# Which buffer holds the weight sums of the last two pairs of column blocks in the second batch's first layer

## The chip, the cores and the metric

The kernel runs on one core of a Trainium2 chip. The metric is the time on the device in microseconds (us), as the median of several runs. One execution was also taken by the hardware profiler; it gives the profile and the trace that are read here. TensorE does matrix products, VectorE (DVE in the profile) and GpSimd (POOL) do operations on tensors, ScalarE (ACT) does copies and activation functions, and SyncE (SP) issues the transfers (DMAs). SBUF is the memory on the core, PSUM holds results of TensorE, and DRAM is the memory off the core.

## The reference

Attention with a mask by cluster is followed by a two-layer network with the activation x·sigmoid(1.702x). Only the second part matters here:

```python
def _moe_ref(x, w_in, w_out) -> np.ndarray:
    h = x @ w_in
    g = h * (1.0 / (1.0 + np.exp(-1.702 * h)))
    return (g @ w_out).astype(np.float32)
```

x has 3072 rows (4 batches of 768 tokens) and 512 columns, w_in is 512 x 2048, and w_out is 2048 x 512. All is float32.

## The kernel before

The kernel has one long first part, the attention of all four batches (until about 340 us of the span), and then the two layers batch after batch (b = 0 to 3). The order of all instructions on each engine is the order in which the program writes them; no scheduler changes it.

**Products by seven.** Both layers multiply by the scheme of Strassen and Winograd: the matrices are cut in 2 x 2 parts, and seven products of sums of these parts take the place of eight products. So sums of weights and sums of inputs have to be made. Batches 0 and 1 use seven products in the first layer. Batches 2 and 3 apply the scheme twice there (`first49`), with 49 products, and need more sums of weights.

**The first layer of batch 1** is the stage of the change (lines 1380 to 1396). It works through eight blocks of 128 hidden columns, in the order TURN = 0, 4, 1, 5, 2, 6, 3, 7. I call the position in this order n, so n = 0 to 7. Two neighbours, n = 0 and 1, n = 2 and 3, and so on, are a pair. For each n the program writes, in this order:

- `first7_psum` (L922): seven products on TensorE (L928), in three banks of PSUM, with additions on VectorE (L884) and copies and gelus on ScalarE (L936, L942, L946, L949) between them. The products take the weight sums S[1], S[2] and S[4] of this n; S[3] lies in the weights' own place.
- for even n from 2 on, `inner_w` (L995) of the pair before: eight operations on VectorE that make the inner sums for the later batches from this pair's S, in the buffer `Zb[4]`, and then four DMAs (L1018), issued by SP, that copy these sums and S itself to DRAM (`kept_i`): 896 KB from `Zb[4]`, then 384 KB of the first S and twice 128 KB of the second S of the pair.
- `sums_w1(n + 2)` (L977): the three weight sums of the block two places later, for n + 2 up to 7. The sums of n = 0 and 1 were made by GpSimd at the end of batch 0; those from n = 2 on are made by VectorE.
- `after7` (L959): one subtraction of the block before, and for blocks f from 4 on four operations of `start_t`.
- two steps of `pend`, which store the rest of batch 0's output while there is any.

After the last n, `after7` and `inner_w` of the last pair follow, and then the second layer (`second49`), with seven groups k = 0 to 6 of seven products.

**Where the sums lie.** `wq` is a ring of two tiles named W (128 partitions x 768 elements). The sums of n = 0 and 1 lie in its two tiles. For n from 2 on a slice of six rows of 128 in `Zb[2]` or `Zb[1]` is used; these are views of `Z_of[2]` and `Z_of[1]`, which the second layer needs for sums of its own weights. They were saved to DRAM (`kept_z`) and are loaded again by `move_z` (L969) in the second layer of batch 1. `1 + n // 2 % 2` gives 2 for n = 2 and 3, 1 for n = 4 and 5, and 2 again for n = 6 and 7.

**Waits.** The program writes no waits by hand. From the tiles that each instruction reads and writes, the language puts in the waits for semaphores: a write to a slice waits for all earlier reads of it, by engines and by DMAs. A new tile of the ring waits for what used the tile two before it. Later users of the ring are `first49` of batches 2 and 3.

On VectorE `sums` always shows as L618, and `add` as L884.

Of the kernel before, what the change touches and what calls it, by code (L numbers as in the profile page):

```python
# [38 lines left out]
def fast(  # L39
# [576 lines left out]
    def sums(engine, todo):  # L616
        for o, a, op, b in todo:
            engine.tensor_tensor(out=o, in0=a, in1=b, op=(  # L618
                ALU.add if op == "+" else ALU.subtract))
# [3 lines left out]
    def A_in(row, col, f):  # L623

        at = (row * FB + f) * P
        return w_in[:, 2 * col:2 * col + 2, at:at + P]
# [350 lines left out]
    def sums_w1(n):  # L977

        if n >= FB:
            return  # L980
        f = TURN[n]
        if n < 2:
            S = wq.tile([P, 3, 2, P], FP32, name="W")
        else:
            S = Zb[1 + n // 2 % 2][:, n % 2 * 6:n % 2 * 6 + 6].rearrange(
                "p (i c) n -> p i c n", c=2)
        w_of[FB + f] = {1: S[:, 0], 2: S[:, 1], 3: A_in(1, 0, f), 4: S[:, 2],
                        0: S}
        S = w_of[FB + f]
        A11, A12, A22 = A_in(0, 0, f), A_in(0, 1, f), A_in(1, 1, f)  # L990
        sums(nc.gpsimd if n < 2 else nc.vector, (
            (S[2], A22, "-", S[3]), (S[1], S[2], "+", A11),
            (S[4], A12, "-", S[2])))
# [385 lines left out]
    for b in range(B):  # L1379
        if b == 1:  # L1380
            done = None
            for n, f in enumerate(TURN):
                made_w = w_of[FB + f][0]
                first7_psum(b, f, *XT)
                if n % 2 == 0 and done:
                    inner_w(*done)
                sums_w1(n + 2)
                if n:
                    after7(TURN[n - 1])
                if n % 2 == 0:  # L1390
                    one = made_w
                else:
                    done = f - FQ, (one, made_w)
                do(pend, 2)
            after7(FB - 1)
            inner_w(*done)
        if b > 1:
            rest = first49(*XT)
        for f in range(FB if b == 0 else 0):
            first7(b, f, *XT)  # L1400
            if f + 2 < FB:
                sums_w(f + 2)
            else:
                sums_w1(f + 2 - FB)
            if f:
                after7(f - 1)
            if b == 0 and f < 3:
                for n in range(3 * f, min(3 * f + 3, FB)):
                    sums_z((nc.gpsimd, nc.vector, nc.vector)[n % 3], n)
            if b == 0 and f in (3, 4):  # L1410
                for i in ORDER[0:4] if f == 3 else ORDER[4:]:
                    turn_w(i)
            if b == 0 and f >= 3:
                for k in {3: (0,), 4: (1, 2), 5: (3,), 6: (4,), 7: ()}[f]:
                    keep_w(k, spare_y())
                if 5 <= f < 7:
                    load_sums(f - 5)
# [510 lines left out]
```

## Time and profile before

| What | us |
|---|---|
| median of three runs | 894.72 |
| lowest, highest | 894.64, 895.08 |
| the profiled execution's own time | 894.73 |
| its span, first to last instruction | 892.6 |
| first layer of batch 1, from its first matmul to the second layer's first | 476.24 to 556.10 |

The profile's times are counted from the start of the span. "Busy" is the time an engine works; the idle time before an instruction is shown together with what ended it, written as <- and the instruction that released it. PEclk is the share of the full clock that TensorE was granted. The chain of waits says what the last instruction waited for, followed back to the beginning. Its first line is

```profile
PE 95%; DVE 2%; DMA 1%; ACT 0%; issue 0%; SPq 0%; DVEq 0%; ACTq 0%
```

So the end of the program is set by TensorE for 95% of the span. The waits of SP's own queue between 500 and 620 us show when the copies of L1018 could be issued:

```profile
SPq L1018 <- DVE Z L618: 53.8, 4, 21.8
SPq L835 <- PE b L1254: 19.3, 4, 7.2
```

The columns after the colon are the total time, the number of waits and the longest. The four waits of L1018 are for the sums that are copied.

### The profile page before, as it was taken

Reading aid. Unit: us, or ns where it says so; the run is one execution under the profiler, and the core shown is the slowest. Engines: PE = TensorE matmul, PEld = TensorE weight load, DVE = VectorE, ACT = ScalarE, POOL = GpSimd, SP = SyncE. Lnnn points to the kernel's source line nnn. Section 1 sums busy time; section 2 is a strip of 40 time slices with the busy share of each in tenths; the row PEclk is TensorE's granted clock in tenths of the full one; section 3 lists DMA queues with packets and bytes.
Section 4 is the critical chain, followed back from the end, with each engine's and each line's share of the span. In section 5 each row is a group of like instructions: output and inputs, shape, how many; then the busy total and the mean of one; then the engine's idle time right before and its main releaser. Section 6 shows DMA issues by size and latency. Waiting matters only on the chain.

```text
span 892.6 us, 18197 instructions
## 1 busy us (share of the span) xinstructions
PE 874.7 (98%) x6910; PEld 605.1 (68%) x6910; DVE 728.1 (82%) x1241; ACT 394.8 (44%) x868; POOL 429.3 (48%) x393
## 2 busy tenths in 40 slices
PE   8999999999999999999999979999999999999996
PEld 3444444444444445557997546999887999887995
DVE  4899898999999996998997645799656899665894
ACT  3677767777777764322112323111444212444211
POOL 6889999999999997693220000134000134000120
PEclk9999999999999999999999999999999999999999
DMA  9755566666655320035643311747511447501523
GB/s 175 134 105 104 103 121 150 140 131 137 137 130 121 86 67 19 0 119 167 224 140 102 98 71 71 282 142 267 141 54 48 166 142 265 171 25 48 185 66 97
DMA packets 183185, 110.48 MB, mean 124 GB/s; under 512 B 153528, under 2 KB 161712, under 8 KB 180528
## 3 DMA queue, kind: packets, MB, share of 16 engines
q1 hardware_dynamic: 182832, 109.09, 45.2%
q8 instruction: 57, 0.93, 0.5%
q14 instruction: 40, 0.33, 0.1%
q10 hardware_dynamic: 256, 0.13, 0.1%
HBM read 83.05 MB, written 26.14 MB: 122 GB/s over the span
## 4 chain that ended last, share of the span: by engine, by line
PE 95%; DVE 2%; DMA 1%; ACT 0%; issue 0%; SPq 0%; DVEq 0%; ACTq 0%
PE b L1254 29%; PE s L492 14%; PE o L557 14%; PE b L1129 8%; PE b L893 8%; PE m L1084 7%; PE b L928 7%; PE s L515 3%; PE m L574 3%; PE m L348 1%; DVE Z L618 1%; DMA in<-in_k_dram 1%; DMA kept_i<-Z 0%; PE s L506 0%; PE o L296 0%
## 5 line engine op out<-in xcount | busy, mean ns | idle before, releaser
L541 POOL TENSOR_TENSOR sum<-sum,A 128x384 f32<-128x384 f32 x252 | 265.3, 1089 | 23.0 <-ACT A L523 21.3
L618 POOL TENSOR_TENSOR Y<-y,Y 128x768 f32<-128x768 f32 x24 | 58.0, 2431 | 392.8 <-DVE y L884 368.9
L523 ACT ACTIVATE A<-s 128x768 f32<-128x768 f32 x192 | 146.2, 808 | 85.8 <-PE s L515 66.3
L492 PE MATMUL s<-T,T 64*64 64x384 f32 x1536 | 143.1, 487 | 0.0
L557 PE MATMUL o<-A,inv 64*64 64x384 f32 x1536 | 141.2, 483 | 0.0
L884 DVE TENSOR_TENSOR G<-b,G 128x384 f32<-128x384 f32 x128 | 68.4, 554 | 53.7 <-PE b L928 30.8
L492 PEld LDWEIGHTS s<-T,T 64*64 64x64 f32 x1536 | 54.9, 132 | 69.1 <-ACT A L523 35.8
L618 DVE TENSOR_TENSOR G<-G 128x768 f32<-128x768 f32 (+1 forms) x84 | 101.1, 1230 | 0.2
L557 PEld LDWEIGHTS o<-A,inv 64*64 64x64 f32 x1536 | 58.3, 133 | 38.4 <-issue 33.3
L1254 PE MATMUL b<-G,w_out 128*128 128x192 f32 x320 | 55.9, 326 | 0.0
L1142 ACT COPY G<-b 128x384 f32<-128x384 f32 x64 | 30.4, 480 | 52.2 <-PE b L1129 52.2
L1254 PEld LDWEIGHTS b<-G,w_out 128*128 128x128 f32 x320 | 52.7, 190 | 1.1
L1254 PE MATMUL b<-E,Wz 128*128 128x192 f32 x288 | 50.3, 326 | 0.0
L1254 PEld LDWEIGHTS b<-E,Wz 128*128 128x128 f32 x288 | 47.3, 190 | 0.3 <-DVE E L618 0.3
L515 PE MATMUL s<-rows,rows 64*64 64x384 bf16 x720 | 45.5, 323 | 0.0
L515 PEld LDWEIGHTS <-rows 64*64 64x64 bf16 x720 | 22.9, 107 | 32.8 <-issue 32.7
L1254 PE MATMUL b<-G,Wz 128*128 128x192 f32 x224 | 41.0, 326 | 0.0
L1254 PE MATMUL b<-G,Z 128*128 128x192 f32 x224 | 39.0, 326 | 0.0
L541 POOL TENSOR_TENSOR sum<-A 128x384 f32<-128x384 f32 x32 | 37.3, 1185 | 0.0
L1254 PEld LDWEIGHTS b<-G,Wz 128*128 128x128 f32 x224 | 37.2, 190 | 0.0
L1254 PEld LDWEIGHTS b<-G,Z 128*128 128x128 f32 x224 | 36.8, 190 | 0.0
L898 ACT ACTIVATE G<-G 128x384 f32<-128x384 f32 x32 | 16.1, 523 | 46.4 <-DVE G L884 44.9
(234 smaller groups left out, 1682.2 us busy)
## 6 DMA issues: line engine op xcount, KB each, us to landing
Wz<-kept_w SPq DMA_DIRECT2D x78, 256.0 KB
Z<-kept_z SPq DMA_DIRECT2D x9, 1024.0 KB
raw<-in_moe_w_in_dram SPq DMA_DIRECT2D x16, 512.0 KB
raw<-in_moe_w_out_dram SPq DMA_DIRECT2D x16, 512.0 KB
Z<-kept_i SPq DMA_DIRECT2D x8, 1024.0 KB
inv<-in_v_dram SPq DMA_DIRECT2D x16, 384.0 KB
in<-in_q_dram SPq DMA_DIRECT2D x60, 96.0 KB
in<-in_k_dram SPq DMA_DIRECT2D x60, 96.0 KB
```

The lines of the kernel that those rows point to most:

```text
L492: nc.tensor.matmul(out=ps[c:c + D, a, 0:HALF], lhsT=T[p, 1][rows, kt * P + c:kt * P + c + D], rhs=T[p, 0][rows, h * HALF:(h + 1) * HALF], ...
L515: nc.tensor.matmul(out=s_of[u][c:c + D, a, :], lhsT=rows_of[1, p % 2][rows, kt * P + c:kt * P + c + D], rhs=rows_of[0, p % 2][rows, h * HA ...
L523: nc.scalar.activation(out=A_of[u], in_=s_of.pop(u), func=AF.Exp, scale=SCALE)
L541: nc.gpsimd.tensor_tensor(out=sum_of[g][:, a], in0=(A_of[u - 1] if kt == 1 else sum_of[g])[:, a], in1=A_of[u][:, a], op=ALU.add)
L557: nc.tensor.matmul(out=o_of[g][a * D:(a + 1) * D, r, 0:HALF], lhsT=v_in[p][rows, a, kt, :], rhs=A[rows, a, :], start=(kt == 0), stop=(kt = ...
L618: engine.tensor_tensor(out=o, in0=a, in1=b, op=(ALU.add if op == "+" else ALU.subtract))
L884: nc.vector.tensor_tensor(out=o, in0=p, in1=a, op=ALU.add)
L893: nc.tensor.matmul(out=ps[:, 0:HALF], lhsT=a[:, c], rhs=x(c), start=(c == 0), stop=(c == 1))
L928: nc.tensor.matmul(out=ps, lhsT=a[:, c], rhs=x(c), start=start and c == 0, stop=(c == 1), skip_group_check=True)
L1084: nc.tensor.matmul(out=whole_of[j][m][:, 0:HALF], lhsT=a[:, c], rhs=x(c), start=n == 1 and c == 0, stop=c == 1, skip_group_check=True)
L1129: nc.tensor.matmul(out=ps[i][:, h * QT:(h + 1) * QT], lhsT=a(o), rhs=M[o][n], start=n in (1, 2, 5) and h == 0, stop=True, skip_group_check ...
L1254: nc.tensor.matmul(out=ps, lhsT=A[n][:, f], rhs=M[n][:, f], start=start and f == 0, stop=(f == FQ - 1), skip_group_check=True)
```

## The change

The sums of n = 6 and 7 are put into the ring `wq` instead of `Zb[2]`. They are made by the same engine as before, since the line that chooses the engine is unchanged.

```diff
         f = TURN[n]
-        if n < 2:
+        if n not in range(2, 6):
             S = wq.tile([P, 3, 2, P], FP32, name="W")
         else:
             S = Zb[1 + n // 2 % 2][:, n % 2 * 6:n % 2 * 6 + 6].rearrange(
                 "p (i c) n -> p i c n", c=2)
```

With this, the sums of n = 6 take the ring's tile that held n = 0, and those of n = 7 the tile that held n = 1. The products of n = 6 and 7, `inner_w` of the last pair and its three copies of S read W instead of `Zb[2]`. The number of instructions on TensorE, VectorE, ScalarE and GpSimd is the same, and so is their order. On SP, the reload of `Z_of[2]` no longer waits for the last pair's three copies of S; the three loads of Wz behind it take over these waits.

## The prediction

> **What bounds the kernel now.** I read the page first, then the busy times of the eight column blocks of the edited stage, then the waits of that stage, then its timeline, one engine after another. The page says that TensorE is the bound almost everywhere:
>
> ```profile
> PE 874.7 (98%) x6910; PEld 605.1 (68%) x6910; DVE 728.1 (82%) x1241; ACT 394.8 (44%) x868; POOL 429.3 (48%) x393
> ...
> PE   8999999999999999999999979999999999999996
> ```
>
> One slice of the 40, the 24th (513 to 536 us), drops to 7. The start, the end and this slice are the only weak ones. Slice 24 lies in the second batch's first layer. I cut this stage at the first matmul of each block n = 0 to 7 (476.24, 485.27, 494.30, 503.33, 513.02, 522.05, 538.03, 547.07, end 556.10) and asked for busy times by stretch; these are n = 2, 3 and 5:
>
> ```profile
> core 0: us, PE busy (x) PEld busy (x) DVE busy (x) ACT busy (x) POOL busy (x), PEclk, DMA share, GB/s
> ...
> 494.30:503.33 9.03, 9.03 (x30) 5.32 (x29) 4.18 (x10) 3.40 (x8) 0.00 (x0) 1.00 0.20 44
> 503.33:513.02 9.69, 9.29 (x29) 5.24 (x28) 7.43 (x20) 3.38 (x8) 0.00 (x0) 1.00 0.42 162
> ...
> 522.05:538.03 15.98, 10.85 (x29) 6.04 (x28) 7.71 (x21) 3.41 (x8) 0.00 (x0) 0.89 0.26 98
> ```
>
> The first number is the length. A block is 9.03 us when TensorE never waits. Blocks 3 and 5 do the same matmuls behind the same kind of VectorE work, yet block 3 takes 9.69 and block 5 takes 15.98. The waits of this stage name one DMA and one long hole:
>
> ```profile
> PE b L928 <- ACT G L949: 5.5, 2, 5.1
> DVE Z L618 <- DMA kept_i<-Z: 4.6, 1, 4.6
> ```
>
> The timeline of TensorE shows the hole in block 5 and its small sister in block 3, and how slowly TensorE resumes (one product is x4 in the records; durations overlap, so I use differences of starts):
>
> ```profile
> 508.49 1.45 PE L928 MATMUL b<-Tx,w_in 128*128 128x384 f32 x4
> 510.34 1.56 PE L928 MATMUL b<-x,Z 128*128 128x384 f32 x4 [0.40 <-ACT G L949]
> 511.73 1.45 PE L928 MATMUL b<-Tx,w_in 128*128 128x384 f32 x4
> ...
> 527.21 1.45 PE L928 MATMUL b<-Tx,w_in 128*128 128x384 f32 x4
> 533.79 2.93 PE L928 MATMUL b<-x,Z 128*128 128x384 f32 x4 [5.13 <-ACT G L949]
> 536.51 1.69 PE L928 MATMUL b<-Tx,w_in 128*128 128x384 f32 x4
> ```
>
> The timeline of all engines at the hole shows the chain that ends it:
>
> ```profile
> 529.34 0.43 DVE L618 TENSOR_TENSOR Z<-w_in 128x256 f32<-128x256 f32 x1 [4.64 <-DMA kept_i<-Z]
> ...
> 532.26 0.55 DVE L884 TENSOR_TENSOR G<-b,G 128x384 f32<-128x384 f32 x1
> 532.85 0.52 ACT L936 ACTIVATE G<-G 128x384 f32<-128x384 f32 x1 [6.25 <-DVE G L884]
> 533.28 0.46 ACT L949 COPY G<-b 128x384 f32<-128x384 f32 x1
> ```
>
> The first row is the first sum of `sums_w1(6)`. It overwrites six rows of `Zb[2]` that hold pair 2's sums (n = 2), and the copy of these rows to DRAM (L1018) was issued only at 524.72, as soon as `inner_w(1)` had finished. Behind it on VectorE stand two more sums, four operations of `after7`/`start_t`, and the addition of L884 at n = 5. ScalarE's gelu waits for that addition, L949's copy stands behind the gelu, and TensorE's product with S[4] (L953) may not write the bank that L949 still reads.
>
> **What the Trainium skill says.** "DMA: Bandwidth & Descriptors", section "Queues, rings and completion order": on a DMA engine the increment of a semaphore lands only after every earlier write of that engine. So the wait for the 384 KB copy also carries the 896 KB copy issued just ahead of it. The trace agrees: by stretches of 1 us the DMA engines moved 229, 423, 354 and 374 kB from 525 on, the two copies are 1311 kB, reached at about 528.8, and VectorE went on at 529.34. "TensorE: Matmul & The Clock Gate", section "Part 1": the array falls to half clock after an idle window of about 3.4 us and returns after a busy one. The trace agrees: after 5.13 us idle it shows 0.50, after 0.40 us none:
>
> ```profile
> 528.60:533.80 5.20, 0.07 (x2) 0.01 (x1) 3.40 (x10) 0.89 (x2) 0.00 (x0) 0.98 0.19 63
> 533.80:536.50 2.70, 2.70 (x4) 1.51 (x5) 0.53 (x1) 0.52 (x1) 0.00 (x0) 0.50 0.00 0
> ...
> 509.00:513.00 4.00, 3.60 (x11) 1.82 (x11) 1.95 (x5) 1.89 (x4) 0.00 (x0) 1.00 0.46 164
> ```
>
> **The change part by part.** (1) Removed: the first sum of `sums_w1(6)` no longer waits for the copy of `Zb[2]`. It now waits for pair 1's copy (n = 0) out of the ring's first place, issued from 506.39 in a row of three. The DMA engines fall idle at 511, after 115 + 401 + 401 + 369 + 286 = 1572 kB by stretches of 1 us, which is all four copies of the pair:
>
> ```profile
> 510.00:511.00 1.00, 0.66 (x2) 0.49 (x3) 0.56 (x1) 0.38 (x2) 0.00 (x0) 1.00 0.87 286
> 511.00:512.00 1.00, 1.00 (x4) 0.57 (x3) 0.07 (x1) 0.43 (x1) 0.00 (x0) 1.00 0.00 1
> ```
>
> That is 13 us before the sum is reached; even with 0.5 us from last byte to release (528.8 to 529.34) it is free. The two other users are earlier still: TensorE's last product with the ring's tiles starts at 491.72, `inner_w(0)` reads them until 504.3. (2) What is late next: VectorE's own work. Block 3 shows it: the same 8 operations of `inner_w`, 3 sums and `after7` without a DMA wait leave a hole of 0.40. On VectorE the two passes run in step, 18.72 us apart: L884 at 502.24 and 520.96, `inner_w` at 502.71 and 521.44. So the first sum, at 505.88 in the first pass, would start at 505.88 + 18.72 = 524.60 instead of 529.34, 4.74 us earlier. (3) On the path: from start to start, block 5 against block 3:
> - last matmul before the hole to first after it: 533.79 - 527.21 = 6.58 against 510.34 - 508.49 = 1.85: 4.73 less (the DMA wait);
> - first group after the hole: 2.72 against 1.39: 1.33 less (half clock);
> - second group to the next block: 538.03 - 536.51 = 1.52 against 513.02 - 511.73 = 1.29: 0.23 less (clock recovering).
>
> Sum 4.73 + 1.33 + 0.23 = 6.29 us, which is 15.98 - 9.69. (4) Moved: the sums for n = 6, 7 are written to W and read from there by TensorE, `inner_w(3)` and three copies. Counts and engines are the same: 6 sums on VectorE at about 0.42 us. VectorE's reads of W (Z<-W, 0.415 to 0.426 us) and of Z (0.414 to 0.426) don't differ. That it writes sums of this shape to W isn't shown; with 128x192 it is, in the next stage: 0.346 to 0.351 us for W, 0.345 to 0.347 for p. I take nothing; the bound is 10% of three sums, 0.13 us, either way. n = 7's first sum waits for the ring's second place, copied with the first, so the same 13 us and more cover it. (5) SP: the reload of `Z_of[2]` (issued 568.46, first used at 583.39 in the fourth product of the second layer) loses its wait on the last pair's copies; the three Wz loads behind it take over those waits, and they wait for TensorE until 573.19 anyway, later than copies issued by 564.27. The reload stays behind that of `Z_of[4]`, so nothing moves; without that cover it would have to slip by some 10 us to matter. The next stage writes the ring's tiles (`first49`) from 622.5, 58 us after the last copy is issued. (6) After 538.03 TensorE is not idle until the last matmuls near 883, and everything follows TensorE, not a fixed time: the 6.29 us should come off whole.
>
> Against the profiled execution's own time, 894.73 (span 892.6 and 2.13 around it): 894.73 - 6.29 = 888.44. The median of the plain runs is 894.72, so I say **888.4**.
>
> **Rivals.**
> A, the forecast, 888.4: 84%. Spread 0.5 either way: 0.13 for W, the rest for the 0.44 us between the lowest and highest run before.
> B, only the wait goes: the clock still dips once in this stage, so the 1.56 us stay. 894.72 - 4.73 = 890.0. For it: block 3 resumes with 1.56 instead of 1.45. Against it: the clock reads 1.00 there. 6%.
> C, more than A: block 5 loses also its 0.66 us beyond 9.03 (n = 6 and 7 show 9.04 and 9.03): 887.8. Against it: those blocks have no 3 sums behind `inner_w`, or none of the 8 operations before them. 4%.
> D, the change doesn't do what it says: the ring's place is released only with the last copy of pair 2. The DMA engines are busy there until 529.6, so release about 530.1, 0.8 us later than now: 895.5, no change that can be told. Against it: the sum's wait in program order is for the semaphore that pair 1's 384 KB copy signals. 3%.
> E, the other side: without its rest of 5 us TensorE is granted a lower clock later. From 538.03 to 883.1 it works 345 us without a hole. At 0.97 this costs 345 x (1/0.97 - 1) = 10.7, less 6.29: 4.4 slower, 899.1. It turns the sign from a mean clock of 0.982 down. For it: the clock does move in this trace (0.50, 0.84). Against it: each long stretch from 538 to 820 reads 1.00, and these follow 60 us and more of full work. 3%.
>
> **How the numbers follow.** The likeliest is A, 888.4. The range reaches from C to B, 887.8 to 890.1, 94%; D and E stay out. A measurement here can't tell less than 0.2% (1.8 us) from no change. A, B and C are faster by more than that: 94%. D is within: 3%. E is slower: 3%.
>
> **What would show it.** After: no VectorE wait for kept_i; a block 5 of 9.7 us with a hole of about 0.4 before the product with S[4]; clock 1.00 through the stage; block 6 starting near 531.7 and the second layer near 549.8; then every later start 6.3 us earlier and a span of 886.3. B shows as 0.5 clock after a short hole, D as a VectorE wait of the old length, E as stretches below 1.00 after 550. A wait of SP or TensorE that isn't in the trace of before would make the sum wrong.

## The result

The changed kernel takes 888.23 us (median of five runs, 888.05 to 888.49). The kernel before takes 895.08 us in the median of the five runs taken with it, the three known ones among them (894.64 to 897.43). The ratio is 0.992, with a 95% interval from 0.9906 to 0.9935. The profiled execution took 888.23 us with a span of 886.1 us; before it was 894.73 with 892.6. The forecast was 888.4.

The page after has the weak slice gone. Its 24th place is now a 9, like its neighbours:

```profile
PE 873.0 (99%) x6910; PEld 604.4 (68%) x6910; DVE 727.3 (82%) x1241; ACT 394.5 (45%) x868; POOL 430.9 (49%) x393
...
PE   8999999999999999999999999999999999999996
```

The busy times by block, again blocks 3 and 5 (the first number is the length, PEclk the granted clock):

```profile
503.33:513.02 9.69, 9.29 (x30) 5.23 (x29) 7.43 (x20) 3.38 (x7) 0.00 (x0) 1.00 0.42 162
...
522.05:531.74 9.69, 9.29 (x30) 5.23 (x29) 7.44 (x20) 3.38 (x8) 0.00 (x0) 1.00 0.42 162
```

Block 5 went from 15.98 to 9.69 us, and the two blocks are now the same in every column but one instruction of ScalarE and the rounding of VectorE's time. The waits of the stage after have no DMA any more, and TensorE's holes sum to 0.8 us:

```profile
PE b L928 <- ACT G L949: 0.8, 2, 0.4
```

The timelines of TensorE and of VectorE at the place of the old hole:

```profile
527.18 1.45 PE L928 MATMUL b<-Tx,w_in 128*128 128x384 f32 x4
529.04 1.56 PE L928 MATMUL b<-x,Z 128*128 128x384 f32 x4 [0.40 <-ACT G L949]
530.43 1.45 PE L928 MATMUL b<-Tx,w_in 128*128 128x384 f32 x4
```

```profile
524.25 0.42 DVE L618 TENSOR_TENSOR Z<-w_in,Z 128x256 f32<-128x256 f32 x1
524.59 0.42 DVE L618 TENSOR_TENSOR W<-w_in 128x256 f32<-128x256 f32 x1
525.04 0.42 DVE L618 TENSOR_TENSOR W<-W,w_in 128x256 f32<-128x256 f32 x1
525.38 0.42 DVE L618 TENSOR_TENSOR W<-w_in,W 128x256 f32<-128x256 f32 x1
```

The first sum follows the inner sums at once (524.59), where it had waited until 529.34. The product after the hole takes 1.39 us from start to start, not 2.72. The second layer begins at 549.78 instead of 556.10, and the last transposes of TensorE (L1313) at 876.62 instead of 882.93, which is 6.31 us earlier. Nothing was given back on the way.

### The profile page after: what moved, and what is told of

Read it like the earlier page. It is cut to its first block, busy times and chain, and to the rows that moved or that the text cites. A ratio compares the mean times of both kernels' runs of the same rounds, so it can differ in the third digit from the quotient of the medians.

```text
span 886.1 us, 18197 instructions
## 1 busy us (share of the span) xinstructions
PE 873.0 (99%) x6910; PEld 604.4 (68%) x6910; DVE 727.3 (82%) x1241; ACT 394.5 (45%) x868; POOL 430.9 (49%) x393
## 4 chain that ended last, share of the span: by engine, by line
PE 95%; DVE 2%; DMA 1%; SPq 1%; ACT 0%; issue 0%; POOL 0%; DVEq 0%; ACTq 0%
PE b L1254 29%; PE s L492 14%; PE o L557 14%; PE b L1129 8%; PE b L893 8%; PE m L1084 7%; PE b L928 6%; PE s L515 3%; PE m L574 3%; PE m L348 1%; DVE Z L618 1%; DMA in<-in_q_dram 1%; SPq L134 0%; DMA short<-in_centroids_dram 0%; DVE G L884 0%
## 5 line engine op out<-in xcount | busy, mean ns | idle before, releaser
L618 POOL TENSOR_TENSOR Y<-y,Y 128x768 f32<-128x768 f32 x24 | 59.8, 2503 | 384.8 <-DVE y L884 357.5
L618 DVE TENSOR_TENSOR G<-G 128x768 f32<-128x768 f32 (+1 forms) x84 | 99.3, 1209 | 0.2
```

Source lines behind the costliest of these rows:

```text
L618: engine.tensor_tensor(out=o, in0=a, in1=b, op=(ALU.add if op == "+" else ALU.subtract))
```

## The experiments

Seven kernels were tried beside the two known ones, and then two of them once more beside the changed kernel. Each time stands beside runs of the kernel before on the same chip. The lengths of block 5, from the profiles, carry most verdicts, since they are free of what the start and the end of the program add.

**Only n = 6 in the ring (only6).**

```diff
-        if n not in range(2, 6):
+        if n in (0, 1, 6):
```

> Only the sums of n = 6 go to the ring; those of n = 7 stay in Zb[2]. My theory: the whole gain is the one wait of the first sum for n = 6, and n = 7's sum is reached near 531.1, about 1 us after the last copy of pair 2 has landed (estimate 530.1 from the DMA engines' end at 529.6). So block 5 takes 9.7 us and the time is 888.2, as with both. Rival 1: n = 7 inherits a part of the wait, some tenths of a us up to 1 us, and block 6 grows by as much. Rival 2: each of the two moves brings half, 891.5.

Measured: 888.31 us (before 895.61, ratio 0.9917, 0.99 to 0.9933). Block 5 takes 9.69 us, block 6 takes 9.03. The sums of n = 7 into `Zb[2]` don't wait. So one of the two moves is the whole change; both rivals fall.

**Only n = 7 in the ring (only7).**

```diff
-        if n not in range(2, 6):
+        if n in (0, 1, 7):
```

> Only the sums of n = 7 go to the ring; those of n = 6 stay in Zb[2]. My theory: no gain, block 5 stays at 16.0 us with a hole of 5.1 us and the time at 894.8 (within 0.3). Rival 2 (each move brings half): 891.5.

Measured: 895.76 us (before 895.61, ratio 1.0002, 0.9993 to 1.0011). The wait and the hole stand as before:

```profile
PE b L928 <- ACT G L949: 5.5, 2, 5.1
DVE Z L618 <- DMA kept_i<-Z: 4.6, 1, 4.6
```

There is no gain, and the hole is 5.12 us, as expected. The time itself is 0.96 us above the 894.8 that was expected (within 0.3), but the kernel before was at 895.61 here too. In this profiled execution block 5 takes 16.71 us, 0.73 more than in that of before. The timeline and the clock by stretches say where these are:

```profile
533.79 2.93 PE L928 MATMUL b<-x,Z 128*128 128x384 f32 x4 [5.12 <-ACT G L949]
536.51 2.42 PE L928 MATMUL b<-Tx,w_in 128*128 128x384 f32 x4
538.76 1.45 PE L928 MATMUL b<-x,w_in 128*128 128x384 f32 x4
```

```profile
528.60:533.80 5.20, 0.08 (x2) 0.01 (x1) 3.41 (x10) 0.89 (x2) 0.00 (x0) 0.79 0.19 64
533.80:536.50 2.70, 2.70 (x4) 1.50 (x5) 0.52 (x1) 0.52 (x1) 0.00 (x0) 0.50 0.00 0
536.50:538.00 1.50, 1.50 (x4) 0.88 (x3) 1.21 (x3) 0.52 (x1) 0.00 (x0) 0.50 0.00 0
538.00:538.76 0.76, 0.76 (x2) 0.33 (x2) 0.76 (x3) 0.00 (x0) 0.00 (x0) 0.71 0.00 0
```

The column before the last two is the clock. It fell to half already inside the hole (0.79 on average there, 0.98 before), and full clock came back only after 538. In the profiled execution of before the stretch from 536.50 already read 0.84:

```profile
536.50:538.00 1.50, 1.50 (x5) 0.91 (x4) 1.21 (x3) 0.52 (x1) 0.00 (x0) 0.84 0.00 0
```

So after the same hole the slow clock cost 1.33 + 0.96 = 2.29 us here (2.72 against 1.39, and 2.25 against 1.29, start to start), and 1.56 there.

How long the half clock lasted can be estimated from these means, if only 1.00 and 0.50 occur: a mean of 0.79 over 5.20 us then holds 2 x 0.21 x 5.20 = 2.18 us at half. Before it is 0.21 + 2.70 + 0.48 = 3.4 us, and in only7 2.18 + 2.70 + 1.50 + 0.44 = 6.8 us, twice as long. Only the part in which TensorE works costs time: 2.70 + 0.48 = 3.18 us before and 2.70 + 1.50 + 0.44 = 4.64 us here. Half of that is 1.59 and 2.32 us, close to the 1.56 and 2.29 measured.

**The wait kept, TensorE kept at work (warm).** In the kernel before, in block n = 5 ahead of the product with S[4] (L953):

```diff
+        if f == TURN[5]:
+            spare = bank()
+            for _ in range(16):
+                nc.tensor.matmul(
+                    out=spare, lhsT=ident_h,
+                    rhs=ident_h[:, None, :].broadcast_to((P, 4, P)),
+                    start=True, stop=True)
         product(v, S[4], lambda c: X[1, 1, c], False)
```

> The kernel before, with 16 matmuls of 128x512 in bf16 that nobody reads added to TensorE in block n = 5, just where the hole is; the wait itself stays. My theory: they take about 3.5 us of the 5.1 us, no idle stretch is long enough for the half clock, and TensorE resumes at 1.00 when the chain lets it. The wait of 4.73 us stays, the 1.56 us of slow clock goes: block 5 takes 14.4 us and the time is 893.2. Rival: the slow first products have another cause (refilling the pipeline), then 894.8. Other rival: the added matmuls delay the real ones, then more than 894.8.

Measured: 893.43 us (before 895.61, ratio 0.9979, 0.9969 to 0.9989). Block 5 takes 14.43 us, where 14.4 was expected.

```profile
528.54 3.62 PE L956 MATMUL m<-ident_h 128*128 128x512 bf16 x16
533.83 1.56 PE L928 MATMUL b<-x,Z 128*128 128x384 f32 x4 [1.68 <-ACT G L949]
535.23 1.45 PE L928 MATMUL b<-Tx,w_in 128*128 128x384 f32 x4
```

VectorE's wait is still 4.64 us, and the product with S[4] starts at 533.83, as it did before (533.79). But it is at full speed from the first matmul on, and the clock reads 1.00 through the whole block:

```profile
522.09:536.52 14.43, 12.76 (x46) 6.81 (x44) 7.54 (x20) 3.38 (x8) 0.00 (x0) 1.00 0.28 109
```

The slow clock is therefore a cost by itself, and idle time is its cause; refilling a pipeline is not, since a hole of 1.68 us doesn't bring it.

**Copies of S first (copyfirst).** The kernel before, `Zb[2]` and all, with the loop of the copies in `inner_w` in another order:

```diff
-        for at, x in ((slice(0, 14), st[:, 0:14]),
-                      (slice(14, 20), S[0].rearrange("p i c n -> p (i c) n")),
+        for at, x in ((slice(14, 20), S[0].rearrange("p i c n -> p (i c) n")),
                       (slice(20, 22), S[1][:, 1]),
-                      (slice(22, 24), S[1][:, 0:3:2, 1])):
+                      (slice(22, 24), S[1][:, 0:3:2, 1]),
+                      (slice(0, 14), st[:, 0:14])):
```

> The kernel before, with Zb[2] for n = 6 and 7 as there, but the three copies of S to DRAM are written ahead of the copy of Zb[4] in the program, so that SP doesn't hold them back until the inner sums are made. My theory: what counts is that the copy has landed when VectorE comes to the sum, not which buffer it is. The copies need only the sums made a pair earlier, so SP can issue them right after the previous pair's, before 512; VectorE then never waits and the time is 888.3, block 5 9.7 us. Rival: the reuse of the buffer itself is bad in another way (TensorE's reads or VectorE's reads just before), then a wait remains and the time is between 889 and 894.8.

Measured: 888.61 us (before 895.61, ratio 0.992, 0.9904 to 0.9937); block 5 takes 9.69 us. The sums of n = 6 are written over the same rows as before the change, right behind the last inner sum:

```profile
525.23 0.42 DVE L618 TENSOR_TENSOR Z<-w_in,Z 128x256 f32<-128x256 f32 x1
525.56 0.42 DVE L618 TENSOR_TENSOR Z<-w_in 128x256 f32<-128x256 f32 x1
```

The copies had landed long before. By stretches of 1 us the DMA engines moved 115 + 452 + 351 + 387 + 268 = 1573 kB between 507 and 512, which is the first pair's inner sums and the second pair's three copies of S, and then almost nothing until 524. So the buffer itself does no harm. What counted was a copy that stood behind another one in SP's order of issue, and that other one needed sums not made yet.

**Less ahead of the copy (dose).** The kernel before again:

```diff
-        for at, x in ((slice(0, 14), st[:, 0:14]),
+        for at, x in ((slice(12, 14), st[:, 12:14]),
                       (slice(14, 20), S[0].rearrange("p i c n -> p (i c) n")),
+                      (slice(0, 12), st[:, 0:12]),
                       (slice(20, 22), S[1][:, 1]),
```

> The kernel before, with the order of the copies in inner_w changed: first two rows of Zb[4] (128 KB, the sum made last), then the 384 KB of the first S, then the other twelve rows of Zb[4], then the rest. So the same wait stays, behind 524 kB instead of 1311 kB. My theory: at 400 kB/us the copy lands 2.0 us earlier, VectorE waits 2.7 instead of 4.6 us, the hole is about 3.2 us. If that is short enough for the clock to stay, block 5 takes 12.5 us and the time is 891.3; if the clock still dips, 892.8. Rival: a wait is a fixed latency of a copy to DRAM, whatever lies ahead of it in the queue; then the wait stays 4.6 us and the time 894.8.

Measured: 893.55 us (before 895.52, ratio 0.9975, 0.9968 to 0.9982); block 5 takes 14.40 us. The waits and TensorE's timeline:

```profile
PE b L928 <- ACT G L949: 3.8, 2, 3.4
DVE Z L618 <- DMA kept_i<-Z: 2.9, 1, 2.9
```

```profile
532.54 2.83 PE L928 MATMUL b<-x,Z 128*128 128x384 f32 x4 [3.40 <-ACT G L949]
535.16 1.92 PE L928 MATMUL b<-Tx,w_in 128*128 128x384 f32 x4
```

The wait fell from 4.64 to 2.92 us, by 1.7 where 2.0 was expected. So it does depend on what lies ahead of the copy, and the rival of a fixed latency falls. The hole fell to 3.40 us, and in this execution that still cost 1.23 + 0.47 = 1.70 us of slow clock. The 20 runs reach from 891.12 to 895.02; three lie between 891.12 and 891.83, where the expectation without slow clock was 891.3, and fifteen above 893. That fits a hole which is just long enough in most runs and not in some. The granted clock of each run, averaged over its span, says the same: the four fastest runs (891.12 to 892.49) read 0.997 or 0.998, as the changed kernel does, and the other sixteen 0.993 to 0.996. Only one execution, a slow-clock one, has a profile. By the same estimate as in only7 (0.53 over the 2.66 us from 532.50, 0.73 over the 1.76 us after them) its half clock lasted 2.50 + 0.95 = 3.45 us, all of it once TensorE worked again; half of that is the 1.70 us. With the slow clock 892.8 was expected; the median is 0.75 above that.

**Sums of n = 6 and 7 on GpSimd (pool67).** In the changed kernel:

```diff
-        sums(nc.gpsimd if n < 2 else nc.vector, (
+        sums(nc.gpsimd if n not in range(2, 6) else nc.vector, (
```

> The changed kernel, with the sums of n = 6 and 7 made by GpSimd instead of VectorE. My theory: with the wait gone, block 5's last 0.66 us over 9.03 is VectorE's own work (8 inner sums, 3 weight sums, 5 more ahead of the addition). Without the 3 sums (1.1 us) the addition comes in time, and block 5 takes 9.03 us: 887.6. GpSimd has nothing else to do there. Rival: VectorE isn't what is late, or it runs slower beside GpSimd; then 888.2 or more.

Measured: 887.55 us (before 895.52, ratio 0.9914, 0.9898 to 0.9931); block 5 takes 9.03 us, and its hole is gone. The timeline of GpSimd also shows when the ring's first place was free:

```profile
510.92 0.73 POOL L618 TENSOR_TENSOR W<-w_in 128x256 f32<-128x256 f32 x1 [55.27 <-DMA kept_i<-W]
```

GpSimd waited for pair 1's copy until 510.92. In the changed kernel VectorE comes to this sum at 524.59, 13.7 us later.

**Inner sums in two halves (split).** In the changed kernel, `inner_w` stops after its first four sums, and the loop takes its second half in the next block:

```diff
+            if n == 0:
+                yield
         for at, x in ((slice(0, 14), st[:, 0:14]),
...
             nc.sync.dma_start(out=kept_i[j, :, at], in_=x)
+        yield
...
                 if n % 2 == 0 and done:
-                    inner_w(*done)
+                    inner = inner_w(*done)
+                if done:
+                    next(inner)
...
-            inner_w(*done)
+            for _ in inner_w(*done):
+                pass
```

> The changed kernel, with inner_w cut in two: its first four sums in the even block, its last four and the copies in the odd block that follows. My theory: VectorE's load is evened out, 1.7 us less ahead of the addition in blocks 3 and 5, so both holes of 0.40 us close and blocks 3 and 5 take 9.03 us: 888.2 - 1.3 = 886.9. The copies are issued some 9 us later but still land before their buffers are needed. Rival: the odd blocks now get a hole of their own, or the later copies bring a wait for the ring back: 888.2 or more.

Measured: 887.62 us (before 895.52, ratio 0.9918, 0.9901 to 0.9934). Blocks 3 to 6 all take 9.03 us, two of them here:

```profile
503.42:512.45 9.03, 9.03 (x29) 5.32 (x28) 5.92 (x16) 3.42 (x8) 0.00 (x0) 1.00 0.00 0
512.45:521.48 9.03, 9.03 (x29) 5.32 (x28) 4.75 (x12) 3.40 (x8) 0.00 (x0) 1.00 0.46 176
```

The second layer begins at 548.57 (549.78 in the changed kernel), and TensorE has no hole from there to the end. VectorE does wait 1.4 us for a copy ahead of the last pair's inner sums, but TensorE doesn't feel it. Even so the median was only 0.6 us under the changed kernel's 888.23, half of what was expected. In this execution 10.08 us pass from the start of the last transposes to the end of the span, against 9.48 in the changed kernel's. So the comparison was made again, in the same rounds.

**The three side by side (after_b, pool67_b, split_b).**

> The changed kernel itself, on the same chip as the two below and in the same rounds. Expected 888.3, with the longest block 9.69 us (blocks 3 and 5). Gain over the kernel before between 6.3 us, which is what the profiled execution of before gives, and 7.3 us, which is what the medians of a larger number of its runs gave; if the half clock after the hole varies in length from run to run, the runs of before spread over about 3 us and those of this one over less than 1.5.

> The changed kernel with the sums of n = 6 and 7 on GpSimd, once more beside the changed kernel. Theory: 0.66 us less than the changed kernel (block 5 at 9.03). Rival: what is gained in the stage is given back later: no difference.

> The changed kernel with inner_w cut in two, once more beside the changed kernel. Theory: 1.33 us less than the changed kernel (blocks 3 and 5 at 9.03), since TensorE stays without a hole to the last matmul. Rival: the copies, issued later, and VectorE's wait of 1.4 us before the last pair's inner sums cost it a part: 0.6 us less, the same as with GpSimd.

| Kernel | median us | lowest, highest | ratio to before (895.43), 95% interval |
|---|---|---|---|
| changed (after_b) | 888.50 | 887.95, 888.85 | 0.992, 0.9907 to 0.9934 |
| GpSimd sums (pool67_b) | 887.42 | 887.28, 887.63 | 0.9909, 0.9894 to 0.9925 |
| halves (split_b) | 887.21 | 887.03, 887.34 | 0.9907, 0.9892 to 0.9922 |

Against the changed kernel this is 1.08 us less with GpSimd (0.66 expected) and 1.29 us less with the halves (1.33 expected). All runs of both lie below all runs of the changed kernel. The profiled executions agree: from the stage's first matmul to the second layer's first they take 73.57 us (after_b), 72.90 (pool67_b) and 72.24 (split_b), which is 0.67 and 1.33 less. The other 0.4 us of GpSimd's gain in the medians are not explained. The halves have the shortest stage, but the times don't tell the two versions apart: their runs overlap here, and in the set before GpSimd's median was the lower one. The end of the program, from the start of the last transposes, takes 9.62 us in split_b's profile, against 10.08 in split's, with the same kernel. So no lasting cost of the later copies shows.

The changed kernel gains 6.93 us here, between the 6.3 and 7.3 that were expected, and spreads over 0.9 us. Before spread over 1.75 us in its nine runs, where about 3 were expected if the slow clock varies in length; its 20 and 23 runs beside the other experiments spread over 2.7 and 3.1 us.

## Why the prediction was right

The forecast case came, at nearly its number: 6.29 us were expected from the profiled executions, and they differ by 894.73 - 888.23 = 6.50. Of these, 6.32 are at the start of the second layer, and 0.03 of that were there at the stage's first matmul (476.24 and 476.21). The other 0.2 us lie behind the last transposes, in the end of the last stores: from L1313's start to the end of the span 9.67 us before, 9.48 after.

- *The wait goes and the ring is free.* Right. only7 shows that the wait of n = 6 alone mattered, pool67 that the place in the ring was free 13.7 us ahead (13 were estimated). The rival that the change does nothing is out.
- *What is late next is VectorE's own work, as in block 3.* Right: 524.59 for the first sum (524.60 forecast), a hole of 0.40, a block of 9.69. pool67 and split show the cause, since taking 3 or 4 operations off VectorE ahead of the addition closes the hole.
- *Three terms, 4.73 + 1.33 + 0.23.* From before to after, the step over the hole went from 6.58 to 1.86, the next from 2.72 to 1.39, and the third from 1.52 to 1.29: right for this pair of profiles. Of the separate parts, warm took out the clock's 1.56 and left the wait (block 5 shorter by 1.55); its counterpart, only the wait gone and the clock still slow (rival B), came in no run.
- *The size against the medians* is the one weak term. The sum took the slow clock from one profiled execution, at 1.33 + 0.23 us. only7, with the same hole, lost 2.29. Larger sets of before had medians of 895.61, 895.52 and 895.43, not 894.72, and against those the changed kernel gains about 7 us. The forecast time of 888.4 doesn't suffer from this, since 894.73 and the 15.98 us of block 5 come from the same execution; the gain of 6.29 us does, and that the median of three runs stood at 894.72 too was luck. That the length of the slow stretch varies is shown by these two profiles. The longer one seems to be the usual one: the profiled execution of before has a mean clock of 0.996 and only7's 0.994, and 41 of the 52 runs of before beside the experiments read 0.992 to 0.994. But that it accounts for the difference of the medians isn't shown: beside only6 the four runs of before at 0.996 are no shorter (median 895.62) than the seven at 0.993 (895.65).
- *Nothing for the moved sums, for n = 7, for SP.* Right. VectorE writes W in 0.42 us as it wrote Z; only6 shows that n = 7's place makes no difference; the reload of `Z_of[2]` is issued at 561.45, 7.0 us earlier than before, and TensorE didn't wait for it in either.
- *A lower clock later (rival E)* didn't come. From 532 to 814 every long stretch after reads a clock of 1.00, among them

```profile
550.00:614.00 64.00, 64.00 (x394) 63.86 (x393) 59.17 (x80) 11.30 (x35) 19.17 (x8) 1.00 0.66 229
...
749.00:814.00 65.00, 65.00 (x314) 53.13 (x313) 39.45 (x84) 27.94 (x52) 0.00 (x0) 1.00 0.27 84
```

- *Block 5 loses its last 0.66 us too (rival C)* did not happen by itself, as said: it took another engine or another order to do it.

## What to carry to other kernels

Writing a buffer again right after its copy to DRAM was issued cost the whole copy here, and also what stood ahead of the copy in the queue (4.64 us behind 896 KB, 2.92 behind 128 KB). Another buffer removed that, and so did issuing the copy before the one that had to wait for newer data. When a stall of one engine makes TensorE idle for several microseconds, count the slow clock after it as well, with a range and not a single value. And look for a sister of the stalled block that does the same work without the wait: its length says what is late next, and here it gave the new length to the hundredth of a microsecond.

## What was not expected of the hardware

The same hole of 5.1 us cost 1.56 us of slow clock in one execution and 2.29 in another, and a hole of 3.40 us cost 1.70. By the estimate given with only7, the clock was at half for about 3.4 us in the first and the last of these, and for 6.8 us in the second. Sixteen matmuls of no use, put into the hole, made the program about 2 us faster in the medians (893.43 against 895.61), with the wait untouched. The end of the program, from the last transposes to the last store, took between 9.44 us (only7) and 10.08 us (split) in kernels in which nothing of it had been changed.
